# Two layers of long convolution and FFN on one core: k before h at the start, k kept by residue, the first FFN unit started row by row, and a new written-out order

## The chip, the cores and the metric

The kernel runs on one core of a Trainium2 chip. The metric is device time in microseconds (us) of one execution; before the change it is 345.2 us, the median of three runs (345.08 to 345.33). The profile below covers 343.4 us of it, from the first to the last instruction; the remaining 1.84 us (345.24 us for the profiled run itself) lie outside the traced span.

## The reference

The input is a sequence of 2048 rows of 512 bf16 values. Two identical layers follow each other; each has an H3 convolution block (A) and a gated FFN (B), both with a layer norm in front and a residual around them:

```python
def _A_ref(q, k, v, shift_k, ssm_k, ssm_D):
    ...
    for t in range(ks):                       # ks = 4 taps
        k_shift = k_shift + k_pad[:, t:t + S, :] * shift_k[:, ks - 1 - t][None, None, :]
    kv = k_shift * v
    # y = causal convolution of kv with ssm_k over all 2048 rows, per channel, by FFT
    ...
    y = y + kv * ssm_D[None, None, :]
    return q * y
def _B_ref(x, w_gate, w_up, w_down):
    return (_silu(x @ w_gate) * (x @ w_up)) @ w_down     # 512 -> 1792 -> 512

x = A_q
x = x + _A_ref(_layernorm(x), A_k, A_v, A_shift_k, A_ssm_k, A_ssm_D)
x = x + _B_ref(_layernorm(x), B_w_gate, B_w_up, B_w_down)
x = x + _A_ref(_layernorm(x), A_k, A_v, A_shift_k, A_ssm_k, A_ssm_D)
x = x + _B_ref(_layernorm(x), B_w_gate, B_w_up, B_w_down)
```

The convolution's result y doesn't depend on x, so it is computed once and used in both layers.

## The kernel before, in words

**Tiling.** The 2048 rows are cut into four blocks of 512. In a block, partition p holds the rows 4p to 4p + 3; the last of these four numbers is the "residue" r. The convolution is done block by block with a transform of length 1024 whose matrices `fwd` and `inv` (sines and cosines) are made on the chip. A block of h (`ssm_k`) and a block of kv go through matmuls with `fwd` into spectra (`ev`, `G`, `H` for h; `X` for kv), VectorE multiplies spectra (`product`), and matmuls with `inv` bring the sum back to rows (`inverse`, `inverse_half` for block 0). The FFN works on units of two residues of one block, 256 rows: 16 units over both layers. A unit's gate and up matmuls take 14 column tiles of 128 with a moving operand of 256 rows, in groups of 4, 4, 4 and 2 tiles; each pair of tiles fills one PSUM bank `pf`, which ScalarE empties (SiLU for the gate, a copy for the up half). VectorE multiplies the two, and matmuls with `wd` add up in `pd`.

**The start, before the first FFN unit.** Everything here belongs to block 0 and to what must be ready for the first unit:

- SyncE issues the loads: h of block 0 (`hn`, `load_h`), then k (`kn`, `load_k`), v, x, h of block 1, v of block 1 and the gate weights. The taps come through ScalarE's queue.
- VectorE makes the phases `ph`, ScalarE takes their sine into `fwd`, and both, with GpSimd, make the 16 diagonal matrices `dg` (identity times one tap).
- TensorE turns h (`transpose_h`, L476, 16 transposes) and k (`transpose_k`, L365, 16 transposes). The turned k goes from PSUM into `kTb` (L371 on ScalarE, L373 on VectorE), where row 4p + r of the block lies at column 4p + r.
- `shift_mul` (L310 with `kTb` and `dg`, 64 matmuls of 128 columns) makes the shifted k; it reads every fourth column of `kTb`. VectorE multiplies by v (L523).
- TensorE transforms h (`half`, L310 with `hs`) and kv (`direct`, L457); ScalarE and VectorE empty the banks (L418, L421). VectorE forms the products (L641, L645) and the sums `m` (L790); TensorE goes back (L796).
- `prologue(0, 0, 0, True)`: VectorE multiplies the normed x by y (L902, L905), adds it to x (L907), takes the statistics of both rows (L808 to L811), GpSimd raises to the power -1/2 (L813), VectorE normalises (`z`, L863), TensorE turns each row (L919, `ptz`), and ScalarE (row 0, L924) and VectorE (row 1, L922) copy it to `zT`. A statistics tile serves both rows, so the power waits for both.
- Then the first unit's gate and up matmuls start. They read both rows of `zT`.

Work of block 1 (h's transposes and spectrum, the shifted k, the spectrum of kv) is put between these on TensorE as a filler.

**What sets the order.** Each operation is registered with `add` on one engine, with a cost and the buffers it reads and writes. `ORDER` holds a rank for each of them; `Plan.order` sorts by rank, deals out ring slots from modelled times, and `Plan.issue` emits in that order. So each engine's program is in the order of the table, and a wrong guess of a cost can't reorder it on the chip. PSUM is in three rings: `pf` 4 banks, `pc` 2, `pd` 2. The ring `pf` serves the spectra, the turned rows, two of the four rows that come back from the inverse, and the gate and up tiles. Where the model sees TensorE idle for more than 0.5 us early on, `issue` puts in dummy matmuls (`wm`).

Of the kernel before, what the change touches and what calls it, by code (L numbers as in the profile page):

```python
# [29 lines left out]
LH0 = 3.6  # L30
LK0 = 4.3
HQ = 'taps'
# [4 lines left out]
KTE = "ADAD"  # L37
# [5 lines left out]
H_SPLIT = False  # L43
PWA = 2.4
# [6 lines left out]
ORDER = [0, 5, 63, 1, 9, 7, 2, 10, 3, 6, 4, 8, 12, 16, 13, 11, 14, 15, 17, 19, 18, 24, 20, 22, 25, 29, 30, 41, 21, 26, 31, 38, 45, 35, 43, 32, 55,  # L51
         42, 51, 64, 74, 59, 71, 100, 104, 70, 76, 23, 27, 28, 37, 53, 39, 65, 44, 36, 34, 50, 58, 69, 72, 47, 40, 33, 46, 56, 62, 48, 61, 49, 60,
         57, 66, 54, 67, 52, 88, 116, 150, 236, 155, 73, 84, 85, 89, 93, 79, 80, 82, 83, 86, 75, 77, 91, 94, 98, 90, 96, 97, 99, 102, 87, 81, 92,
         101, 95, 106, 110, 144, 170, 165, 185, 109, 113, 105, 107, 112, 111, 114, 118, 103, 108, 68, 78, 115, 120, 119, 123, 139, 130, 121, 124,
         127, 125, 129, 132, 140, 142, 148, 134, 138, 141, 154, 158, 161, 136, 146, 152, 117, 122, 128, 126, 133, 137, 143, 145, 160, 147, 173, 178,
         168, 163, 177, 174, 151, 156, 131, 135, 176, 180, 162, 189, 164, 183, 169, 175, 205, 211, 149, 172, 218, 222, 190, 202, 153, 157, 159, 166,
         179, 195, 167, 171, 188, 197, 182, 184, 186, 187, 192, 194, 207, 225, 199, 209, 198, 248, 216, 191, 204, 196, 203, 206, 200, 208, 210, 214,
         215, 219, 226, 230, 237, 224, 228, 233, 231, 241, 246, 256, 249, 258, 262, 275, 274, 280, 277, 283, 287, 291, 296, 292, 298, 299, 302, 309,
         313, 318, 319, 323, 245, 239, 252, 261, 255, 257, 271, 265, 201, 213, 221, 212, 223, 229, 181, 193, 217, 220, 227, 250, 326, 329, 294, 301,
         285, 289, 235, 244, 238, 284, 312, 324, 264, 268, 293, 305, 332, 339, 345, 347, 354, 350, 330, 232, 242, 438, 300, 279, 310, 320, 328, 336,  # L60
         358, 367, 388, 400, 418, 408, 424, 433, 452, 448, 459, 470, 463, 467, 466, 471, 486, 491, 530, 534, 472, 483, 535, 529, 561, 600, 612, 638,
         234, 240, 251, 263, 259, 270, 243, 260, 254, 267, 276, 304, 286, 247, 253, 266, 272, 278, 282, 281, 303, 306, 321, 317, 273, 311, 297, 308,
         290, 295, 269, 288, 315, 327, 333, 314, 322, 307, 316, 325, 331, 335, 334, 338, 343, 359, 352, 361, 340, 351, 337, 344, 362, 368, 370, 348,
         357, 360, 371, 363, 380, 374, 383, 394, 406, 402, 356, 376, 378, 391, 389, 401, 382, 395, 405, 411, 414, 393, 407, 398, 410, 415, 422, 420,
         426, 423, 429, 341, 346, 342, 349, 353, 364, 365, 366, 369, 372, 375, 379, 384, 381, 385, 387, 390, 396, 399, 403, 404, 409, 444, 458, 441,
         456, 462, 464, 474, 476, 478, 484, 489, 497, 492, 499, 503, 505, 517, 526, 514, 518, 436, 447, 446, 451, 428, 445, 425, 430, 481, 510, 494,
         450, 477, 455, 469, 460, 473, 475, 490, 500, 522, 516, 480, 501, 442, 457, 468, 487, 434, 439, 506, 533, 528, 502, 509, 488, 520, 524, 537,
         539, 546, 544, 551, 685, 580, 386, 419, 435, 461, 449, 482, 485, 511, 504, 519, 531, 555, 559, 542, 554, 560, 563, 571, 574, 581, 585, 437,
         496, 397, 413, 498, 513, 540, 527, 545, 548, 578, 589, 590, 593, 604, 607, 631, 667, 616, 618, 377, 373, 412, 355, 432, 421, 443, 427, 532,
         550, 562, 565, 493, 495, 508, 523, 521, 525, 541, 553, 453, 465, 507, 512, 572, 567, 610, 597, 583, 605, 632, 622, 536, 479, 440, 392, 538,  # L70
         591, 602, 599, 629, 623, 416, 595, 431, 454, 515, 614, 626, 635, 640, 658, 662, 651, 645, 690, 694, 720, 723, 697, 703, 727, 730, 698, 701,
         708, 719, 706, 716, 734, 741, 733, 736, 752, 747, 771, 767, 762, 764, 692, 417, 696, 816, 650, 643, 655, 670, 665, 684, 688, 715, 781, 777,
         788, 792, 814, 800, 822, 830, 837, 861, 866, 869, 874, 880, 875, 879, 894, 896, 876, 882, 889, 892, 888, 893, 904, 937, 923, 942, 954, 948,
         961, 966, 973, 984, 1000, 1037, 557, 569, 547, 556, 573, 579, 564, 568, 586, 596, 624, 587, 598, 603, 611, 592, 606, 577, 584, 619, 634,
         639, 543, 549, 570, 575, 552, 558, 566, 576, 594, 637, 659, 601, 609, 582, 588, 617, 646, 666, 649, 669, 677, 680, 683, 630, 647, 648, 654,
         656, 661, 636, 642, 664, 672, 678, 641, 657, 627, 633, 613, 625, 608, 644, 660, 681, 686, 663, 673, 620, 628, 653, 671, 615, 621, 676, 687,
         691, 674, 679, 668, 675, 682, 689, 695, 693, 699, 702, 704, 709, 710, 721, 722, 732, 700, 712, 742, 770, 761, 735, 753, 729, 738, 749, 756,
         717, 726, 759, 786, 779, 744, 750, 754, 768, 740, 748, 758, 763, 773, 790, 783, 774, 780, 766, 784, 787, 793, 796, 797, 801, 804, 705, 711,
         707, 713, 714, 718, 725, 724, 728, 731, 739, 745, 737, 746, 751, 755, 760, 765, 769, 772, 776, 807, 812, 810, 813, 820, 823, 829, 835, 832,
         842, 844, 848, 852, 850, 854, 856, 858, 865, 870, 878, 868, 872, 839, 845, 819, 825, 824, 831, 799, 827, 815, 821, 834, 860, 863, 828, 838,  # L80
         805, 811, 847, 851, 836, 853, 859, 867, 871, 802, 806, 809, 817, 855, 864, 833, 840, 873, 881, 886, 849, 862, 841, 846, 877, 895, 890, 907,
         917, 1054, 946, 743, 778, 782, 789, 785, 791, 795, 826, 883, 900, 908, 915, 918, 911, 919, 922, 925, 936, 938, 941, 940, 950, 885, 891, 898,
         920, 929, 930, 965, 976, 972, 981, 988, 994, 999, 1001, 1003, 1009, 1018, 1021, 1034, 1045, 1036, 1040, 757, 652, 794, 775, 803, 808, 798,
         818, 843, 857, 979, 986, 978, 982, 910, 914, 901, 913, 897, 905, 884, 887, 947, 951, 991, 996, 1004, 1010, 1013, 1007, 1029, 1015, 997,
         1041, 963, 1025, 983, 955, 1061, 969, 1055, 1069, 927, 1052, 1066, 1035, 1022, 1064, 1068, 1085, 1093, 1113, 1098, 1105, 1118, 1142, 1144,
         1148, 1153, 1147, 1151, 1181, 1185, 1168, 1172, 1155, 1158, 1170, 1173, 1174, 1179, 1160, 1162, 1188, 1195, 1199, 1204, 1208, 1202, 1110,
# [24 lines left out]
R = 4  # L111
# [126 lines left out]
def kernel(  # L238
# [168 lines left out]
    def spectrum(name):  # L407
        return new("s8", name, [P, 4, 2, D], parts=8)
# [878 lines left out]
```

## Time and profile before

| what | value |
|---|---|
| time | 345.2 us (345.08 to 345.33) |
| span of the profile | 343.4 us |
| TensorE busy | 338.5 us, 99% |
| VectorE busy | 279.8 us, 81% |
| ScalarE busy | 254.1 us, 74% |
| GpSimd busy | 38.9 us, 11% |
| gate and up matmuls, 896 + 896 | 111.0 + 110.9 us |
| down matmuls, 462 | 105.5 us |
| granted TensorE clock | 1.000 |

A matmul's row in the profile lasts from its start to its modelled end, and the next one starts before that end. Eight gate matmuls of 256 columns are listed as 1.04 us, yet the next group starts 0.87 us after the first began. So what a matmul costs is read from the distance of starts, not from the sum of durations: 0.109 us for 256 columns, 0.216 us for 512, 0.056 us for 128. The same holds to a lesser degree for the other engines: a VectorE operation listed with 0.41 us may be followed by the next 0.34 us after its start. For the order of things at the start, the timeline of each engine and the busy time in chosen stretches are used.

### The profile page before, as it was taken

To read this page: it belongs to the slowest core of one execution; us is meant where nothing else is said; L and a number is where in the kernel's file an instruction comes from. 1 tells how busy PE (TensorE), PEld (TensorE's weight loads), DVE (VectorE), ACT (ScalarE), POOL (GpSimd) and SP (SyncE) were. 2 spreads that over 40 slices of the span, in tenths; PEclk is the share of its full clock that TensorE was granted. 3 is DMA by queue.
4 is the path that set the end of the run, shared out by engine and by line. 5 is a ranking of instruction groups with operands and counts; after the bars stand their busy time and mean duration, and the time that the engine had idled before them with its cause. 6 is when DMAs were issued, how large, how long until landed. Compare 5 with 4: busy or idle time off the path is not lost.

```text
span 343.4 us, 6604 instructions
## 1 busy us (share of the span) xinstructions
PE 338.5 (99%) x2616; PEld 248.2 (72%) x2616; DVE 279.8 (81%) x479; ACT 254.1 (74%) x503; POOL 38.9 (11%) x46
## 2 busy tenths in 40 slices
PE   8999999999999999999999999999999999999996
PEld 6656868777588657778587767767686877777683
DVE  8899999999999997999999999979998524535112
ACT  7999988989888538977699997569774635556362
POOL 4100110102111001212020001111101000100000
PEclk9999999999999999999999999999999999999999
DMA  7999212091110154132101020510102120101100
GB/s 273 325 298 313 47 31 63 15 166 34 34 46 17 40 95 113 26 63 67 32 10 38 2 76 2 128 26 1 32 0 50 27 36 0 25 8 27 41 12 32
DMA packets 42089, 22.96 MB, mean 67 GB/s; under 512 B 33861, under 2 KB 39882, under 8 KB 42058
## 3 DMA queue, kind: packets, MB, share of 16 engines
q1 hardware_dynamic: 41904, 22.47, 26.5%
q8 instruction: 20, 0.33, 0.4%
q14 instruction: 11, 0.09, 0.1%
q10 hardware_dynamic: 154, 0.07, 0.1%
HBM read 12.33 MB, written 2.10 MB: 42 GB/s over the span
## 4 chain that ended last, share of the span: by engine, by line
PE 96%; ACT 1%; DMA 1%; SPq 0%; issue 0%
PE pf L310 57%; PE pd L985 28%; PE ps L310 7%; PE ps L457 2%; DMA kn<-in_A_k_dram 1%; PE ps L796 1%; PE pd L944 1%; ACT X L418 0%; PE pt L365 0%; ACT hs L486 0%; ACT H L418 0%; PE ptz L919 0%; ACT n L858 0%; SPq L341 0%; PE pt L476 0%; ACT xc L998 0%
## 5 line engine op out<-in xcount | busy, mean ns | idle before, releaser
L310 PE MATMUL pf<-zT,wg_sb 128*128 128x256 bf16 x896 | 111.0, 273 | 0.0
L310 PE MATMUL pf<-zT,wu_sb 128*128 128x256 bf16 x896 | 110.9, 273 | 0.0
L985 PE MATMUL pd<-wd_sb,ht 128*128 128x512 bf16 (+1 forms) x462 | 105.5, 373 | 0.0
L310 PEld LDWEIGHTS <-wu_sb 128*128 128x128 bf16 x896 | 87.7, 98 | 17.4
L310 PEld LDWEIGHTS <-wg_sb 128*128 128x128 bf16 x896 | 87.7, 98 | 16.3 <-issue 0.3
L965 ACT ACTIVATE sg<-pf 128x512 bf16<-128x512 f32 x112 | 65.3, 603 | 24.3 <-PE pf L310 20.3
L969 ACT CAST ht<-pf 128x512 bf16<-128x512 f32 x112 | 65.0, 594 | 23.5 <-PE pf L310 19.8
L985 PEld LDWEIGHTS <-ht 128*128 128x128 bf16 x462 | 45.2, 98 | 42.7
L972 DVE TENSOR_TENSOR ht<-ht,sg 128x1024 bf16<-128x1024 bf16 (+1 forms) x64 | 39.3, 620 | 24.8 <-ACT ht L969 17.3
L813 POOL TENSOR_TENSOR rstd<-ve,nhalf 128x2 f32<-128x2 f32 x24 | 27.7, 1156 | 206.6 <-DVE ve L811 206.6
L808 DVE BATCH_NORM_STATS2 bnst<-xc 128x6 f32<-128x512 bf16 x48 | 31.5, 684 | 1.9 <-ACT xc L1011 1.3
L1021 ACT CAST dn<-pd 128x512 bf16<-128x512 f32 x24 | 13.5, 594 | 21.5 <-PE pd L985 21.5
L1024 DVE TENSOR_TENSOR xc<-xc,dn 128x1024 bf16<-128x1024 bf16 x12 | 8.3, 689 | 18.7 <-ACT dn L1021 18.5
L652 DVE TENSOR_TENSOR t<-X,G 128x2048 bf16<-128x2048 bf16 x18 | 21.9, 1216 | 0.1
L656 DVE TENSOR_TENSOR t<-X,G 128x2048 bf16<-128x2048 bf16 x18 | 21.9, 1217 | 0.0
L418 ACT ACTIVATE X<-ps 128x512 bf16<-128x512 f32 x32 | 19.0, 610 | 1.3 <-PE ps L457 0.7
L418 ACT ACTIVATE H<-ps 128x512 bf16<-128x512 f32 x24 | 13.9, 607 | 1.7 <-PE ps L310 1.5
L839 POOL TENSOR_TENSOR rstd<-ve,nhalf 128x2 f32<-128x2 f32 x8 | 7.7, 958 | 64.8 <-ACT ve L837 64.8
L664 DVE TENSOR_TENSOR t<-t,t 128x2048 bf16<-128x2048 bf16 x12 | 14.7, 1221 | 0.1
L666 DVE TENSOR_TENSOR Z<-Z,t 128x2048 bf16<-128x2048 bf16 x12 | 14.6, 1219 | 0.1
L310 PE MATMUL ps<-hs,fwd 128*128 128x512 bf16 x40 | 12.5, 379 | 0.3 <-ACT H L418 0.3
L603 ACT ACTIVATE ka<-kTb,tapF 128x512 bf16<-128x512 bf16 x16 | 12.4, 787 | 0.0
(109 smaller groups left out, 325.5 us busy)
## 6 DMA issues: line engine op xcount, KB each, us to landing
hn<-in_A_ssm_k_dram SPq DMA_DIRECT2D x4, 512.0 KB, 6.0
vt<-in_A_v_dram SPq DMA_DIRECT2D x4, 512.0 KB, 6.4
xc<-in_A_q_dram SPq DMA_DIRECT2D x4, 512.0 KB, 3.7
out_dram<-xc SPq DMA_DIRECT2D x15, 128.0 KB, 1.8
wg_sb<-in_B_w_gate_dram SPq DMA_DIRECT2D x1, 1792.0 KB
wu_sb<-in_B_w_up_dram SPq DMA_DIRECT2D x1, 1792.0 KB, 8.2
wd_sb<-in_B_w_down_dram SPq DMA_DIRECT2D x1, 1280.0 KB, 11.7
kn<-in_A_k_dram SPq DMA_DIRECT2D x1, 512.0 KB, 4.5
```

The lines of the kernel that those rows point to most:

```text
L310: nc.tensor.matmul(o, lhsT=lhsT, rhs=rhs, start=(n == 0), stop=(n == len(terms) - 1))
L418: add("ACT", act(D), lambda: nc.scalar.activation(out=view(), in_=ps.t[:], func=ACT.Copy, scale=scale), r=[ps], w=[(buf, keys)], conv=conv)
L652: dve(n * D, lambda t1=t1, part=part: nc.vector.tensor_mul(out=t1.t[:], in0=x.t[:, sl, 0, :], in1=g.t[:, sl, part, :]), [(x, key(slots, (0 ...
L656: dve(n * D, lambda t2=t2, part=part: nc.vector.tensor_mul(out=t2.t[:], in0=x.t[:, sl, 1, :], in1=g.t[:, sl, 1 - part, :]), [(x, key(slots ...
L664: dve(n * D, lambda t1=t1, t2=t2, comb=comb: nc.vector.tensor_tensor(out=t1.t[:], in0=t1.t[:], in1=t2.t[:], op=comb), [t2], [t1], conv=conv)
L666: dve(n * D, lambda t1=t1, part=part: nc.vector.tensor_add(out=z.t[:, sl, part, :], in0=z.t[:, sl, part, :], in1=t1.t[:]), [t1], [zk], con ...
L808: add("DVE", 0.6, lambda st=st, i=i: nc.vector.bn_stats(out=st.t[:], in_=xs[c].t[:, i, :]), r=[(xs[c], (i,))], w=[st])
L813: add("POOL", pw, lambda: nc.gpsimd.tensor_tensor(out=rstd.t[:], in0=ve.t[:], in1=nhalf.t[:].to_broadcast((P, n)), op=ALU.pow), r=[ve, nha ...
L965: add("ACT", act(D), lambda ps=ps, o=o, sg=sg: nc.scalar.activation(out=sg.t[:, o:o + 2, :], in_=ps.t[:], func=ACT.Silu), r=[ps], w=[(sg, ...
L969: add("ACT", act(D), lambda ps=ps, o=o, ht=ht: nc.scalar.copy(out=ht.t[:, o:o + 2, :], in_=ps.t[:]), r=[ps], w=[(ht, (o // 2,))], due=(uni ...
L972: dve(n * W, lambda sg=sg, ht=ht: nc.vector.tensor_mul(out=ht.t[:], in0=ht.t[:], in1=sg.t[:]), [sg], [ht], due=(unit, k / pairs, 0.0, "h"))
L985: nc.tensor.matmul((pds[o] if not cs.start else pds[HP]).t[:, cs], lhsT=ht.t[:, q, o * P:(o + 1) * P], rhs=wt["d"].t[:, ft, cs], start=(ft ...
```

## The change

It has four parts, all but the last in the first 33 us of the kernel.

1. **k first.** `HQ = 'tapsk'`: SyncE issues k's load, then h's. k is turned ahead of h.
2. **k by residue.** `kTb` of block 0 becomes [128, 4, 4, 129]: for each residue its 128 rows in a run, with one zero column ahead. The copies out of PSUM become straight copies without a stride, and all four go to VectorE (`KTE = 'DDDD'`; before, two were on ScalarE). The 64 matmuls read a run of 128 columns instead of every fourth.
3. **The first FFN unit row by row.** The statistics of the two rows in the first prologue are split (`PST = True`): a tile, a variance and a power for each row. In the first unit alone, the first four PSUM tiles (`FS = 4`) of gate and up are each made in two halves of eight matmuls, one for each row (128 columns instead of 256), which wait only for their own row of `zT`.
4. **A new order.** Several costs in `add` are changed (they move nothing by themselves), and `ORDER` is a new table for all 1577 operations (1571 before).

New switches `K_SPLIT`, `VE_DVE`, `H1E`, `YD` and the branch `X0 == "mix"` stay at values that leave the emitted work as it was.

```diff
-LH0 = 3.6
-LK0 = 4.3
-HQ = 'taps'
+LH0 = 4.35
+LK0 = 3.5
+HQ = 'tapsk'
-KTE = "ADAD"
+KTE = 'DDDD'
+FS = 4
+PST = True
...
-ORDER = [0, 5, 63, 1, 9, 7, 2, 10, 3, 6, 4, 8, 12, 16, 13, 11, 14, 15, 17, 19, 18, 24, 20, 22, 25, 29, 30, 41, 21, 26, 31, 38, 45, 35, 43, 32, 55,
...
+ORDER = [0, 6, 55, 1, 2, 5, 11, 13, 3, 8, 4, 10, 16, 19, 9, 12, 14, 15, 17, 23, 18, 21, 20, 22, 24, 28, 27, 34, 25, 29, 35, 51, 56, 49, 53, 57, 67,
...
-        kT[b] = new("k", "kTb", [P, KD, PADL + L], parts=KD + 1)
-        add("POOL", 0.2, lambda: nc.gpsimd.memset(kT[b].t[:, :, 0:PADL], 0.0), w=[(kT[b], (KD,))], due=-48)
+        kT[b] = new("k", "kTb", [P, KD, R, P + 1], parts=KD + 1)
+        add("POOL", 0.2, lambda: nc.gpsimd.memset(kT[b].t[:, :, :, 0:1], 0.0), w=[(kT[b], (KD,))], due=-48)
...
-            dst = lambda dt=dt: kT[b].t[:, dt, PADL:PADL + L].rearrange("d (p r) -> d p r", r=R)
-            src = lambda pt=pt: pt.t[:].rearrange("d r p -> d p r")
+            dst = lambda dt=dt: kT[b].t[:, dt, :, 1:P + 1]
+            src = lambda pt=pt: pt.t[:]
...
+            def at(dt, s):
+                if b:
+                    return kT[b].t[:, dt, PADL + s:PADL + s + R * (P - 1) + 1:R]
+                return kT[b].t[:, dt, s % R, 1 + s // R:1 + s // R + P]
...
-                    mm(ps.t[:, dt * P:(dt + 1) * P],
-                       [(kT[b].t[:, dt, PADL + r - j:PADL + r - j + R * (P - 1) + 1:R], dg.t[:, dt, j, :])
-                        for j in range(KS)])
+                    mm(ps.t[:, dt * P:(dt + 1) * P], [(at(dt, r - j), dg.t[:, dt, j, :]) for j in range(KS)])
...
-        st = ln_stats(c, rows, 0.85)
+        sts = [ln_stats(c, [i], 0.85) for i in rows] if PST else [ln_stats(c, rows, 0.85)] * HP
...
-            zop = normalise(z, (0,), lambda z=z: z.t[:], c, i, o, st)
+            zop = normalise(z, (0,), lambda z=z: z.t[:], c, i, 0 if PST else o, sts[o])
...
+                    split = unit == (0, 0, 0) and 2 * k + (which == "u") < FS
+                    ps = new("pf", "pf", [P, D], F32, parts=HP)
+
+                    def part(ps=ps, o=o, which=which, fts=fts, i=0):
+                        for q in (0, 1):
+                            ft = fts[o + q]
+                            mm(ps.t[:, q * W + i * P:q * W + (i + 1) * P],
+                               [(wt[which].t[:, kd, ft * P:(ft + 1) * P], zT.t[:, kd, i]) for kd in range(KD)])
...
+                    if split:
+                        for i in range(HP):
+                            add("PE", pe(2 * KD, P), lambda part=part, i=i: part(i=i), r=[(zT, (i,)), wt[which]], w=[(ps, (i,))], due=due)
+                    else:
+                        add("PE", pe(2 * KD, W), go, r=[zT, wt[which]], w=[ps], due=due)
...
-            h0 = load_h(0, "SP", -70)
-            k0 = load_k(0, -69.9, after=[h0])
+        else:
+            k0 = load_k(0, -70)
+            h0 = load_h(0, "SP", -69.9, after=[k0])
+            k0 = h0
```

Matched to the operations in the order of registration, the two tables give these programs for TensorE at the start (`hT`, `kT`: four transposes each; `H`: two matmuls of 512 columns; `conv rX dtY`: four of 128):

```text
before: hT r1, r2, r0, r3 | kT 0, 1, 3, 2 | H a1, a0, b1, c1 | conv r0 dt0, r2 dt0, r2 dt1, r1 dt0-3, r0 dt1-3, r3 dt0, r2 dt2-3, r3 dt1-3 | H c0, b0 | X ...
after:  kT 0, 3, 1 | hT r2, r0, r3 | kT 2 | hT r1 | H b0, a0, a1 | conv r2 dt0, r1 dt0, r0 dt0-1, r3 dt0, r1 dt1, r3 dt1, r0 dt2-3, r1 dt2-3, r3 dt2, r2 dt1-3, r3 dt3 | H c0, c1, d0 | X ...
```

and these ahead of the first FFN matmuls (`conv1`: 16 of 128; `id`: x added through the identity; `X1`: spectrum of the next block):

```text
before: ... conv1 r3, inverse s1 r2p1, zT1, zT0, id0, X1, X1, id1 | g 0.2, g 1.0, g 0.0, u 0.2 ...
after:  ... conv1 r3, id0, inverse s1 r2p1, zT0, id1, zT1, X1, X1 | g 0.2 row 0, u 0.2 row 1, g 1.0, u 0.2 row 0, g 0.2 row 1 ...
```

## The prediction

> **What bounds the kernel now.** I read the engines' shares first, then the waits of TensorE, then busy time by stretch, then TensorE's timeline by distance of starts.
>
> The page's shares, and the whole answer to "who waited" for TensorE's matmuls:
>
> ```profile
> PE 338.5 (99%) x2616; PEld 248.2 (72%) x2616; DVE 279.8 (81%) x479; ACT 254.1 (74%) x503; POOL 38.9 (11%) x46
> PE wm L1253 <- DVE wz L1037: 1.1, 1, 1.1
> PE ps L310 <- ACT H L418: 0.3, 1, 0.3
> PE pt L365 <- DMA kn<-in_A_k_dram: 0.3, 1, 0.3
> ```
>
> TensorE is the bound, and it waits only at the start. The change gives it no less to do, so it can win only slots in which TensorE does nothing useful. Where are they? Adding up the distances of starts over the whole timeline, with 0.216, 0.109 and 0.056 us for 512, 256 and 128 columns, leaves nothing unexplained from 33.23 us to the last matmul at about 341 us. All lost slots lie ahead of 33.23. Busy time by stretch (stretch, its length, then busy us of TensorE, its weight loads, VectorE, ScalarE, GpSimd, then clock, DMA share, GB/s):
>
> ```profile
> 5.80:21.75 15.95, 15.95 (x145) 10.20 (x146) 14.39 (x29) 14.63 (x33) 2.41 (x6) 1.00 1.10 304
> 21.75:25.70 3.95, 3.52 (x28) 1.98 (x27) 3.92 (x10) 3.95 (x9) 0.00 (x0) 1.00 1.02 389
> 31.20:33.23 2.03, 1.98 (x18) 0.96 (x15) 2.03 (x5) 2.03 (x6) 0.00 (x0) 1.00 1.58 318
> 33.23:341.00 307.77, 307.19 (x2323) 227.22 (x2322) 250.02 (x405) 224.89 (x443) 33.50 (x30) 1.00 0.19 41
> ```
>
> The useful matmuls from 4.44 (h's first transpose) to 33.23 (first FFN matmul) are 76 of 512 columns and 184 of 128: 76 x 0.216 + 184 x 0.056 = 16.4 + 10.3 = 26.7 us in 28.8 us. So 2.1 us are lost, and TensorE's timeline shows where:
>
> ```profile
> 4.44 1.08 PE L476 MATMUL pt<-ident,hn 128*128 128x128 bf16 x16
> 5.80 1.07 PE L365 MATMUL pt<-ident,kn 128*128 128x128 bf16 x16 [0.28 <-DMA kn<-in_A_k_dram]
> ...
> 8.43 3.74 PE L310 MATMUL ps<-dg,kTb 128*128 128x128 bf16 x64
> 12.01 1.03 PE L310 MATMUL ps<-hs,fwd 128*128 128x512 bf16 x4
> ...
> 23.44 0.28 PE L1253 MATMUL wm<-wz 128*128 128x128 bf16 x2
> 24.02 0.38 PE L310 MATMUL ps<-hs,fwd 128*128 128x512 bf16 x1 [0.30 <-ACT H L418]
> 24.50 0.38 PE L796 MATMUL ps<-m,inv 128*128 128x512 bf16 x1
> ...
> 31.21 0.38 PE L796 MATMUL ps<-m,inv 128*128 128x512 bf16 x1
> 31.62 0.72 PE L919 MATMUL ptz<-ident,z 128*128 128x128 bf16 x8
> ```
>
> (a) 4.44 to 5.80: 16 transposes need 0.9, so about 0.5 goes on waiting for k. (b) 21.75 to 25.7: 0.18 + 0.58 (dummies and a wait for ScalarE) + 0.26 + 0.14 = 1.1 to 1.2, with VectorE (3.92 of 3.95) and ScalarE (3.95 of 3.95) both full. (c) 31.2 to 33.2: 0.2 for z, 0.12, 0.18 before the first gate matmul, 0.5 together. From the last matmul to the span's end is 2.4 us, which the change doesn't touch. So the most it can win is about 2.1 us.
>
> **What the Trainium skill says.** "TensorE: Matmul & The Clock Gate", section "Wait — 56ns, not 53.3ns?": warm matmuls follow each other after N/2.4 GHz + 2.5 ns, 55.6 ns at 128 and 215.7 at 512; the distances above agree. Same page, "Step-by-step: what each phase is for": matmuls stay in program order and only weight loads are pulled ahead, so one waiting matmul holds all behind it; the trace agrees at 24.02. "VectorE: DVE Perf Modes", "Mode 2×_1P — pack two bf16 into one 32-bit read": two results a cycle need 16-bit data of step 1. The strided copy of k and the straight one of h, both from PSUM, agree:
>
> ```profile
> 6.36 0.41 DVE L492 COPY hs<-pt 128x512 bf16<-128x512 bf16 x1
> 6.69 0.67 DVE L373 COPY kTb<-pt 128x512 bf16<-128x512 bf16 x1
> ```
>
> "DMA: Bandwidth & Descriptors", "Queues, rings and completion order": descriptors of one queue are consumed in ring order. h issued at 0.74 is in use at 4.43, k issued at 1.26 at 5.80; swapped, I take k at about 4.3 and h at about 5.8, since both must be through before the second can be used and they are 512 KB each.
>
> **The change part by part.**
>
> *k first.* Until the second load, TensorE can do only transposes. Before these were 16 of h; in the new order 12 of k, since `kT 2` stands behind three groups of h. With the second load at the same 5.8, 4 x 0.056 = 0.22 us more is lost. If h comes 0.2 earlier it is nothing; if its shorter runs make it 0.3 later, 0.5.
>
> From 5.8: 16 transposes of h and 4 of k (1.1), three H pairs (1.3), so the shifted k starts at 8.2 instead of 8.43. Is its input there? VectorE does tapF, neg, dg01, tapT, dg10, two copies of k, dg11, hs r0 (6.7), two dg, kTb 2 (7.4), three dg (8.0), hs r1, kTb 1 (8.7). Group 1 needs dg00 at 8.0, and group 4 (8.87) needs kTb 1 at 8.7 and a semaphore: just in time. The first v product, which needs nine groups of 0.224, comes at 10.3 against 10.20. So VectorE's long chain starts no earlier: four v products end at 13.0, ev c1 (0.64, before done at 9.3) takes it to 13.6, where G starts; before G started at 13.55 after waiting 0.65. The moved ev is hidden in that wait.
>
> *k by residue.* Four copies at 0.34 to 0.41 on VectorE, 1.4 to 1.6, for two at 0.67 there and two on ScalarE (1.07 together). VectorE's wait of 0.87 ahead of 10.20 hides the 0.1 to 0.3; ScalarE's 1.0 only lengthens its wait for x at 9.63 (0.32 before). The 64 matmuls stay at 0.056. Nothing on the path.
>
> *The middle, by the new order.* Chaining the rows' distances through the three programs: X s3 ends at 21.3, the second turn of h1 at 21.7 (before, the same work and one more matmul were done at 21.75). The next matmul, H1 r0, needs ScalarE's copy of h1; ScalarE's list from 12.3 (four ev, seven X at 0.5 to 0.55, the second square 0.84, three small ones 0.8, n1 0.75, h1 0.95) reaches it at about 21.8, so TensorE waits 0.2. With every row at its full listed length ScalarE reaches it at 22.5 and the wait is 0.7; I take 0.2. The sum `m s0+` comes at 21.9, before the inverse wants it at 22.4, and `conv1` r2 and r0 (0.9 each) stand behind it as filler where before there were dummies. VectorE reaches `n*y` at 26.25 (26.43 before). TensorE ends `conv1 r3` and the inverse at 31.0, against 31.43. So of the 1.1 to 1.2 lost in (b) some 0.2 stays: 1.0 won.
>
> *Rows apart.* One more variance on VectorE (0.09 to 0.17) and one more power (0.8 to 1.0 on GpSimd, idle). z0's power is done early, so z follows the v products without the 0.25 wait: z0 at 30.85, z1 ends at 31.6; TensorE waits 0.3 for z0, and after zT1 two X1 pairs fill until row 0 of `zT` is copied (32.2). The first gate half can start at about 32.4. Row 1's copy on VectorE now stands behind two v products (ends 32.65), while the first half runs until 32.85. Of (c) 0.1 is won. Each split tile costs 16 x 0.0558 - 8 x 0.1092 = 0.02, four 0.08; the first tile's SiLU comes later than with one piece, but `pf` tiles are freed just in time (the seventh at 37.7, wanted at 37.9).
>
> *After the first unit* the order is new but the work isn't, and the last stretch above has no slack to win and none lost.
>
> Sum: -1.0 (b) - 0.1 (c) + 0.2 (a) + 0.1 (split) = -0.8 us. **344.4 us.**
>
> **The rivals.**
>
> *A, forecast, 42%:* as above, 344.4.
>
> *B, no change, 30%:* h lands late (+0.5 in (a)) or ScalarE's copy of h1 comes at 22.5 (+0.5). Then the gain in (b) is given back: with one of them -0.8 + 0.5 = -0.3 (344.9), with both -0.8 + 1.0 = +0.2 (345.4). For it: ScalarE is full from 19 to 31 in the trace, and TensorE has no wait to spare.
>
> *C, slower, 20%:* both of B, and the wait is passed on: VectorE is a chain without gaps from 13.55 to 31.15, so a late X or h1 moves z, the 0.7 at h1 pulls behind it H1 and the inverse, and `pf` banks become short in the first unit (0.5 more). -0.8 + 3 x 0.5 = +0.7, 345.9; a new wait of 0.4 after 33 us would make it 346.3. Against it: in the trace a full VectorE never stopped TensorE after 33 us.
>
> *D, all of it, 8%:* nearly all lost slots go and k comes early: -1.8 to -2.0, 343.3.
>
> **How the numbers follow.** The likeliest is A, 344.4. The range leaves out D's end and C's: 343.5 to 346.0. Faster by over 0.2% (below 344.5) are A and D, 0.50; same is B, 0.30; slower C, 0.20.
>
> **What would show it.** Right: TensorE's first FFN matmul near 32.4 and everything after it unchanged; k's transposes at about 4.3 and h's at 5.8; no dummies between 21 and 25, one short wait near 21.8; `kTb` copies at 0.41. Wrong: h landing well after 5.8 and TensorE waiting longer than 0.7 there; matmuls waiting for ScalarE's h1 or H1 by 0.5 or more; any wait of TensorE after 33 us, which would void the claim that only the start matters; or a first FFN matmul that moves while the end doesn't.

## The result, and the profile after

After the change the kernel takes 346.93 us (median of 6 runs, 346.38 to 347.42) against 345.32 us before (6 runs beside it, 345.08 to 346.22). The ratio is 1.0042, 95% interval 1.0028 to 1.0057: it got slower by about 0.4%, where 344.4 us, a gain, was forecast. The profiled spans are 345.4 us after and 343.4 us before.

I read the same views in the same order as before. First the page's shares, and then the whole answer to "who waited" for TensorE's matmuls (us in total, times, longest), now of the kernel after:

```profile
PE 337.5 (98%) x2616; PEld 248.8 (72%) x2649; DVE 277.8 (80%) x482; ACT 252.0 (73%) x501; POOL 39.8 (12%) x47
```

```profile
PE pf L317 <- DMA zT<-z: 1.7, 2, 0.9
PE wm L1305 <- DVE wz L1076: 1.0, 1, 1.0
PE ptz L946 <- DVE z L890: 0.3, 1, 0.3
```

The first of the waits is new, and it is nearly the whole of what was lost: TensorE waits twice for the transfer that turns normed rows into `zT`. The waits for k and for ScalarE's `H` are off this list (the wait for the second load isn't gone: four dummies stand in it, as the timeline below shows). One trap is in the shares: 2649 weight loads but only 2616 matmuls. The 33 missing matmul records show up in the timeline as gaps of one slot (0.22 us, about one every 10 us), in which nothing was lost. They also make TensorE's busy time look smaller than it was.

Busy time by the same stretches as before (stretch, its length, then busy us of TensorE, its weight loads, VectorE, ScalarE, GpSimd, then clock, DMA share, GB/s), kernel after:

```profile
5.80:21.75 15.95, 15.79 (x142) 10.02 (x142) 13.94 (x32) 13.16 (x30) 2.16 (x4) 1.00 1.09 318
21.75:25.70 3.95, 3.86 (x47) 2.92 (x47) 3.92 (x10) 3.95 (x7) 0.00 (x0) 1.00 1.01 395
31.20:33.23 2.03, 1.75 (x21) 1.27 (x21) 2.03 (x7) 2.03 (x7) 0.14 (x1) 1.00 0.70 129
33.23:341.00 307.77, 304.58 (x2311) 225.72 (x2338) 247.77 (x403) 223.79 (x443) 33.78 (x30) 1.00 0.19 41
```

The stretch 21.75 to 25.70 is fuller (3.86 for 3.52), as forecast. The last stretch, where no slot was missing before, has lost 2.6 us of busy time. Part of that is missing records (27 more loads than matmuls in it), so the loss itself has to be read from TensorE's timeline. The start of the kernel after:

```profile
4.14 1.47 PE L379 MATMUL pt<-ident,kn 128*128 128x128 bf16 x12
5.40 0.63 PE L1305 MATMUL wm<-wz 128*128 128x128 bf16 x4
6.09 0.85 PE L494 MATMUL pt<-ident,hn 128*128 128x128 bf16 x12
6.78 0.39 PE L379 MATMUL pt<-ident,kn 128*128 128x128 bf16 x4
7.00 0.39 PE L494 MATMUL pt<-ident,hn 128*128 128x128 bf16 x4
7.33 1.46 PE L317 MATMUL ps<-hs,fwd 128*128 128x512 bf16 x5
8.62 3.74 PE L317 MATMUL ps<-dg,kTb 128*128 128x128 bf16 x64
...
23.50 1.95 PE L317 MATMUL ps<-dg,kTb 128*128 128x128 bf16 x32
25.29 0.38 PE L317 MATMUL ps<-hs,fwd 128*128 128x512 bf16 x1
25.75 0.81 PE L819 MATMUL ps<-m,inv 128*128 128x512 bf16 x3
...
31.64 0.40 PE L946 MATMUL ptz<-ident,z 128*128 128x128 bf16 x4 [0.28 <-DVE z L890]
...
32.75 0.61 PE L317 MATMUL pf<-zT,wg_sb 128*128 128x128 bf16 x8
```

h can be used from 6.09, where before the second load (k) could be used from 5.80. (The first twelve transposes of k start 0.106 us apart, where the transposes of h in the kernel before were 0.056 apart. Nothing is lost by it, since they are done at 5.40, before h has come.) In the middle the 32 matmuls of the shifted k stand where dummies stood, and one wait of 0.24 is left (25.29 to 25.75, less a slot), for VectorE's sum `m`. The first FFN matmul starts at 32.75 instead of 33.23. So at this point the change is 0.48 us ahead, and yet the last matmul of all starts at 342.06 instead of 340.15. The two places where the rest went, in the same view:

```profile
50.05 2.75 PE L1024 MATMUL pd<-wd_sb,ht 128*128 128x512 bf16 x12
53.66 1.05 PE L317 MATMUL pf<-zT,wg_sb 128*128 128x256 bf16 x8 [0.86 <-DMA zT<-z]
...
130.25 0.59 PE L317 MATMUL ps<-vt,fwd 128*128 128x512 bf16 x2
131.66 1.59 PE L317 MATMUL pf<-zT,wg_sb 128*128 128x256 bf16 x13 [0.82 <-DMA zT<-z]
```

Twelve matmuls of 0.216 from 50.05 are done at 52.64, two from 130.25 at 130.68. The next starts at 53.66 and 131.66. By distance of starts TensorE loses 1.03 and 0.98 us. In the kernel before, the matmuls at the same two places follow at once:

```profile
50.20 2.75 PE L985 MATMUL pd<-wd_sb,ht 128*128 128x512 bf16 x12
52.79 1.04 PE L310 MATMUL pf<-zT,wu_sb 128*128 128x256 bf16 x8
...
129.32 0.59 PE L310 MATMUL ps<-vt,fwd 128*128 128x512 bf16 x2
129.75 1.04 PE L310 MATMUL pf<-zT,wu_sb 128*128 128x256 bf16 x8
```

The full account of TensorE in these two traces, by three marks (first spectrum matmul of h, first FFN matmul, last matmul):

| stretch | before | after | difference |
|---|---|---|---|
| to the first `ps<-hs,fwd` | 6.71 | 7.33 | +0.62 |
| from there to the first FFN matmul | 26.52 | 25.42 | -1.10 |
| from there to the last matmul | 306.92 | 309.32 | +2.40 |
| sum (start of the last matmul) | 340.15 | 342.06 | +1.9 |

Of the +2.40, the waits are 1.03 + 0.98. Another 0.33 goes within the first unit (0.08 for the 64 shorter matmuls, and short gaps of 0.06, 0.10 and 0.09 at 38, 43 and 46 us).

### The profile page after: what moved, and what is told of

The parts are those of the page before. It is cut to its first block, busy times and chain, and to the rows that moved or that the text cites. A ratio compares the mean times of both kernels' runs of the same rounds, so it can differ in the third digit from the quotient of the medians.

```text
span 345.4 us, 6633 instructions
## 1 busy us (share of the span) xinstructions
PE 337.5 (98%) x2616; PEld 248.8 (72%) x2649; DVE 277.8 (80%) x482; ACT 252.0 (73%) x501; POOL 39.8 (12%) x47
## 4 chain that ended last, share of the span: by engine, by line
PE 83%; DVE 9%; ACT 3%; DMA 2%; issue 1%; DVEq 0%
PE pf L317 51%; PE pd L1024 25%; PE ps L317 5%; DMA zT<-z 2%; DVE t L664 1%; DVE m L562 1%; PE wm L1305 1%; DVE Z L668 1%; ACT sg L1004 1%; ACT X L436 1%; DVE G L603 1%; PE pt L379 0%; ACT ht L1008 0%; ACT z L885 0%; DVE vt L537 0%
## 5 line engine op out<-in xcount | busy, mean ns | idle before, releaser
L317 PE MATMUL pf<-zT,wg_sb 128*128 128x256 bf16 (+1 forms) x912 | 110.6, 271 | 1.7 <-DMA zT<-z 1.7
L317 PE MATMUL pf<-zT,wu_sb 128*128 128x256 bf16 (+1 forms) x912 | 111.5, 271 | 0.3
L1024 PE MATMUL pd<-wd_sb,ht 128*128 128x512 bf16 (+1 forms) x442 | 101.2, 373 | 1.1
L1008 ACT CAST ht<-pf 128x512 bf16<-128x512 f32 x112 | 63.9, 592 | 21.4 <-PE pf L317 21.2
L1011 DVE TENSOR_TENSOR ht<-ht,sg 128x1024 bf16<-128x1024 bf16 (+1 forms) x64 | 39.4, 620 | 32.4 <-ACT sg L1004 20.4
L836 POOL TENSOR_TENSOR rstd<-ve,nhalf 128x2 f32<-128x2 f32 (+1 forms) x25 | 25.9, 1036 | 213.7 <-DVE ve L834 213.7
L866 POOL TENSOR_TENSOR rstd<-ve,nhalf 128x2 f32<-128x2 f32 x8 | 10.4, 1294 | 59.3 <-ACT ve L864 59.3
L626 ACT ACTIVATE kc<-kTb,tapF 128x512 bf16<-128x512 bf16 x16 | 12.6, 803 | 0.0
```

The source lines that it names most:

```text
L317: nc.tensor.matmul(o, lhsT=lhsT, rhs=rhs, start=(n == 0), stop=(n == len(terms) - 1))
L626: add("ACT", 0.66, lambda j=j, t=t, h=h, dt=dt: nc.scalar.activation(out=t.t[:, h, :, dt], in_=kT[b].t[:, dt, PADL - j:PADL - j + L].rearr ...
L836: add("POOL", pw, lambda: nc.gpsimd.tensor_tensor(out=rstd.t[:], in0=ve.t[:], in1=nhalf.t[:].to_broadcast((P, n)), op=ALU.pow), r=[ve, nha ...
L1008: add("ACT", act(D), lambda ps=ps, o=o, ht=ht: nc.scalar.copy(out=ht.t[:, o:o + 2, :], in_=ps.t[:]), r=[ps], w=[(ht, (o // 2,))], due=(uni ...
L1011: dve(n * W, lambda sg=sg, ht=ht: nc.vector.tensor_mul(out=ht.t[:], in0=ht.t[:], in1=sg.t[:]), [sg], [ht], due=(unit, k / pairs, 0.0, "h"))
L1024: nc.tensor.matmul((pds[o] if not cs.start else pds[HP]).t[:, cs], lhsT=ht.t[:, q, o * P:(o + 1) * P], rhs=wt["d"].t[:, ft, cs], start=(ft ...
```

## What held the second row up: two suspects

The first wait is the strange one. SyncE's queue around it, kernel after:

```profile
48.32 2.50 SPq L919 DMA_TRANSPOSE zT<-z  x2
50.87 1.60 SPq L403 DMA_DIRECT2D xc<-in_A_q_dram  x1
```

The two turns of `zT` (transposed DMA transfers, one for each row of the unit) are issued at 48.32 and 49.6, as before (48.09), and are wanted at 52.64, as before (52.79). The view of times to landing lists only 2.4 us for them, yet TensorE starts at 53.66. What held it up is to be seen in the single packets, from the trace's DMA records of the kernel after (start, duration in us, queue, bytes):

```text
50.656  1.444  q8  instruction  16384
51.395  1.504  q1    256
51.422  1.475  q1    256
51.433  1.466  q1    256
51.499  1.406  q1    256
51.518  1.385  q1      4
...     (13 such packets; the last starts at 51.668; all end at 52.90 to 52.91)
```

The other small packets of this turn have a median of 0.018 us and none takes over 0.06. Thirteen take 1.24 to 1.50 and end together at 52.90, 0.8 us before TensorE starts. The one other transfer that lasts, and that is under way when all of them start, is a fetch of 16 KB of instructions (50.66 to 52.10). "Runtime: NRT & Kernel Launch" of the Trainium skill, section "Instruction fetch mechanics", says that an engine's program comes in blocks of 16 KiB, 256 instructions, over a DMA queue of its own, and that the cost of crossing into the next is "mostly hidden". The trace agrees on the size. The question here is not that cost but what the fetch does to another transfer. The profile's page has 20 such fetches in all. 20 x 256 is close to the 5298 loads and matmuls of TensorE's program, so I take them to be TensorE's. "DMA: Bandwidth & Descriptors" of the same Trainium skill, section "Queues, rings and completion order", says that a DMA engine serves the queues that have work for it in turn, a packet at a time. That fits thirteen packets held up at once on one DMA engine, but the records don't name the engine, so this last step is argued. The traces do tie the packets to the fetch by time. Over all traces of this document there are nine places near 48 and 67 us where packets of a turn take more than 0.2 us. In each of them a fetch of 0.92 to 1.57 us is under way, and the held packets end 0.76 to 0.84 us after the fetch does. What fills these 0.8 us isn't shown. A hold also isn't a loss yet. In the kernel after, the next fetch (68.99 to 69.91) holds packets of the second unit's turn until 70.72 to 70.75, and TensorE loses nothing there.

Before, the fetch in question came at 55.3, after the turn had landed. The change puts 66 more loads and matmuls (64 of the split, one dummy pair) into TensorE's program before this point.

*Theory:* the fetch falls on the turn, and that is the wait at 52.6. In the new order the split brought it there. *Rival:* the new order makes the turn late, and the fetch is a bystander. The wait at 130 seems to have an explanation of its own, in the order of SyncE's queue there, kernel after:

```profile
124.10 2.20 SPq L367 DMA_TRANSPOSE kTb<-in_A_k_dram  x1
126.47 0.45 SPq L403 DMA_DIRECT2D xc<-in_A_q_dram  x1
127.02 1.19 SPq L919 DMA_TRANSPOSE zT<-z  x1
```

z was ready at 122.9, but the turn stands behind two loads and lands 4.6 us after its issue (median of all turns: 2.5). Before, it was issued at 121.16, ahead of both loads (127.43 and 127.81).

## The experiments

A ratio is always to the kernel before, formed from runs beside each other on one chip. It isn't the quotient of the two medians given, which lump rounds together. Where the fetch lies is read from the DMA records. "Lost" is the distance of starts less the matmul's slot.

### The split alone in the old kernel

```diff
 before, with its own order and h first
+FS = 4          (gate and up tiles 0 and 1 of the first unit, a half for each row)
 dummies (29):
-matmul(t[:], lhsT=wz.t[:], rhs=wz.t[:])                         x n
+matmul(t[0:104, 0:104], lhsT=wz.t[:, 0:104], rhs=wz.t[:, 0:104])  x 5n/4
```

> The kernel before with one part of the change, the row-by-row split of the first four gate and up tiles, in the old order; the dummies at the start are 104 columns wide instead of 128 and a quarter more in number, so that they take the same time and TensorE's instruction stream is 76 instructions longer (64 by the split, 12 by the dummies). Theory F: TensorE's 16 KB instruction fetch at 55.3 us moves to about 50.4, onto the transposed load of the second unit's zT (its packets run from 49.2 to 51.5), and TensorE waits 0.3 to 0.9 us for zT near 52.9: 345.7 to 346.3 us. Theory O, that the waits for zT come from the new order alone: no such wait, only the split's 0.1: 345.4 us.

Measured: 345.81 against 345.63, ratio 0.9996 (0.9977 to 1.0016). The fetch came at 54.2, not at the 50 it was steered to, so this run missed its target and can't speak for or against the theory. It does size the split: from the first FFN matmul to the last it is 307.00 us for 306.92, so the shorter matmuls cost 0.08 us, and no wait follows after 33 us.

### The turn ahead of the loads

```diff
 SyncE near 124 us, kernel after, by ORDER:
-kTb <- in_A_k_dram ; xc <- in_A_q_dram ; zT <- z
+zT <- z ; kTb <- in_A_k_dram ; xc <- in_A_q_dram
```

> The changed kernel with one edit in SyncE's order: the transposed load of zT that is issued at 127.0 us, behind the transposed load of k's last block and the load of x, goes ahead of these two. Theory Q, that zT stands in the queue behind the 0.5 MB of k and 0.5 MB of x: the wait of 0.8 to 1.0 us at 130.7 goes, 345.9 to 346.1 us, and the wait at 52.6 stays. Rival, that TensorE arrives there too early for z whatever the queue: the wait stays, 346.9 us.

Measured: 346.86 against 345.63, 1.0033 (1.0019 to 1.0046). The wait at 130 is gone. The wait at 52 stays (1.19; fetch at 51.0), and the traced run has a new one of 0.39 at 71.7, where the next fetch (68.3, 1.57 long) meets the turn of the second unit (issued 67.47). So the wait at 130 goes when the turn goes ahead of the loads, but curing it alone recovers little: the 345.9 to 346.1 expected was missed, and the time is the rival's, though its reason is not.

### The fetch moved, without touching the change

```diff
 dummies of the kernel after:
-t = psp.tile([P, P], ...);      for _ in range(n):             matmul(t[:], lhsT=wz.t[:], rhs=wz.t[:])
+t = psp.tile([P, 2 * P], ...);  for _ in range((n + 1) // 2):  matmul(t[:], lhsT=wz.t[:, 0:P], rhs=wz.t[:])
```

The dummies fill the same time with half as many instructions. A second version has 512 columns and a quarter as many; a third 104 columns and a quarter more, which should bring the fetch forward; a fourth joins the first with the turn ahead of the loads.

> The changed kernel with its early dummies 256 columns wide instead of 128 and half as many, so that TensorE's instruction stream is some 30 instructions shorter. Nothing else changes. Theory F, that the instruction fetch that starts at 50.66 us holds up one DMA engine's part of zT: the fetch comes about 2 us later, the wait of 0.9 to 1.0 us at 52.6 goes, 345.9 to 346.1 us, and the wait at 130.7 stays. Rival, that z is simply made too late for TensorE: the wait stays at 0.5 or more, 346.5 to 346.9 us.

> The changed kernel with both edits: zT ahead of k and x in SyncE's order, and the dummies twice as wide and half as many. Theories F and Q together: no wait for zT over 0.3 us, 344.9 to 345.2 us, slightly below the kernel before, since the first FFN matmul comes 0.5 us earlier and 0.3 us of it is given back in the first unit. If the two waits are passed on to other places: 346 us or more.

> The changed kernel with its early dummies 512 columns wide and a quarter as many, some 44 instructions fewer in TensorE's stream (30 fewer in the run with 256 columns). Theory F: the fetch comes at 55 us or later, no wait for zT near 52.6, and the time is that of the run with 256 columns, 0.4 to 0.5% below the changed kernel. If it was the form of the dummies and not the length of the stream that helped there, the two differ.

> The changed kernel with its early dummies 104 columns wide and a quarter more in number, some 14 instructions more in TensorE's stream. Theory F: the fetch near 50.7 comes about 1 us earlier, 49.5 to 50.5, still on zT's two transposed loads (49.2 to 51.5): the wait stays, 0.4 to 1.0 us, and the time is within 0.15% of the changed kernel. If any change of the dummies removed the wait, it would be gone here too.

> The changed kernel itself, beside the others on one chip, with a second trace. Theory F (the instruction fetch holds up a transposed load of zT): its fetch lies again within 1.5 us of 50.7 us and TensorE waits 0.5 to 1.2 us for zT near 52.6; 0.3 to 0.5% slower than before. If the first trace caught a rare coincidence, no such wait, and the time lies elsewhere.

| version | time, before beside it | ratio (95%) | fetch | lost at 52 | lost at 130 |
|---|---|---|---|---|---|
| after itself, again | 347.40, 345.91 | 1.0034 (1.0018 to 1.0049) | 51.3 | 1.12 | 1.14 |
| dummies 256 wide | 345.40, 345.63 | 0.9988 (0.9976 to 1.0001) | 55.1 | none | 0.64 |
| dummies 512 wide | 345.58, 345.91 | 0.9992 (0.9974 to 1.0009) | 55.3 | none | 0.75 |
| 256 wide, turn first | 345.40, 345.63 | 0.9982 (0.9967 to 0.9997) | 56.1 | none | none |
| dummies 104 wide | 345.86, 345.91 | 1.0003 (0.9988 to 1.0018) | 48.7 | 0.09 | none |

The useful work and its order are the same in the first, second, third and fifth row; only the dummies differ, by 14 to 46 instructions of 5300. The wait at 52 is there with the fetch at 51.3, is down to 0.09 at 48.7, and is absent at 55.1 and 55.3. That shows the theory's first half: the place of the fetch decides. The versions with 256 columns moved the fetch by more than the 2 us expected: alone, the change is 0.5 us below its expectation, while with the turn first, at 345.40, it is just above it (345.2 at most). The 104-wide version missed its expectation (the wait was to stay), and usefully: the fetch came so early that it held twelve packets at the end of the first turn (until 50.64) and was over before the second turn's packets ran. Its trace is of one of the shortest of its twelve runs (344.80, their median 345.86), so it doesn't show what the longer ones lose.

The waits of TensorE with both cures, whole answer:

```profile
PE wm L1304 <- DVE wz L1075: 1.2, 1, 1.2
PE ptz L945 <- DVE z L889: 0.3, 1, 0.3
```

### The split undone

```diff
-FS = 4
+FS = 0
 (each tile at the place of its later half in ORDER; k first, k by residue, statistics by row kept)
 second version, in addition: zT <- z ahead of kTb and xc on SyncE near 124 us
```

> The changed kernel with the split of the first unit's tiles alone undone (FS = 0: each tile in one piece of 256 columns, at the place of its later half); k first, k by residue, statistics by row and the order are kept. TensorE's program has 64 fewer loads and matmuls together ahead of 52 us. Theory (the split's instructions bring TensorE's instruction fetch onto the second row's zT): the fetch lies at 54 to 57 us, the wait at 52.6 is gone, the time is about 345.4 (ratio to before 0.998 to 1.001), and the first FFN matmul starts some 0.4 later than 32.75. Rival (the new order itself brings the wait, wherever the fetch lies): a wait of 0.8 or more at 52 to 54 us stays and the time is 346.5 or more. The wait at 130 is another cause and may stay, 0.6 to 1.0, in both.

> The same without the split, and with SyncE's turn of the second row's zT near 127 us put ahead of the loads of k and x. Theory: no wait at 52 and none at 130; the time is 0.0 to 0.9 below the version without the split alone, about 345.0 (0.997 to 1.000). If the split is worth anything apart from its fetch, this is slower than the version with the fetch moved and the turn first (0.9982) by up to 0.3 us; if it is worth nothing, the same. Rival (order): slower than before, with a wait of 0.8 or more at 52 us.

Measured: 346.21 against 345.75, 1.0018 (1.0010 to 1.0026), and with the turn first 345.47, 0.9997 (0.9989 to 1.0005). TensorE's timeline without the split:

```profile
50.08 2.75 PE L1023 MATMUL pd<-wd_sb,ht 128*128 128x512 bf16 x12
52.67 1.04 PE L316 MATMUL pf<-zT,wg_sb 128*128 128x256 bf16 x8
```

With the split away the fetch is at 55.2 and the gate matmuls follow at once, in the new order. The rival of the first half falls. (In the old order neither the split nor 58 more dummy instructions, below, brought the fetch there: 54.2 and 53.3. So it takes the split together with the rest of the new program.) The first time was above what I expected (1.001 at most), since the wait at 130 was still the full 0.98. The pair of runs sizes that wait, too: its cure takes 1.0018 to 0.9997, 0.7 us, and the intervals don't meet. From the first FFN matmul to the last the second version has 306.92 us, the very figure of the kernel before.

### The fetch alone, without the split

```diff
 dummies of the kernel before, and of the version without the split and with the turn first:
-matmul(t[:], lhsT=wz.t[:], rhs=wz.t[:])                       x n
+matmul(t[0:64, 0:64], lhsT=wz.t[:, 0:64], rhs=wz.t[:, 0:64])  x 2n
```

> The kernel before, with nothing of the change in it: its 29 dummy matmuls of 128 columns at the start become 58 of 64 columns, which is the same time and 58 more loads and matmuls in TensorE's program, close to the 64 that the split adds. Theory (the place of the instruction fetch is enough to cost the time): if the fetch near 50 us falls between 50.6 and 51.3, TensorE waits 0.8 to 1.2 for the second row's zT at 52.8 and the time is above before (1.001 to 1.004); if it falls elsewhere (it did so once in an old-order kernel with such an addition: 54.2), no wait and 0.999 to 1.001. Rival (the wait belongs to the new order, the fetch only happens to lie there): no wait in either case.

> The version without the split and with the turn first (0.9997, no wait after 33 us in its profile), with the dummies likewise 60 of 64 columns in place of 30 of 128. Theory: with the fetch between 50.6 and 51.3 the wait for the second row's zT at 52 is back, 0.8 to 1.2, without any split, and the ratio goes up to 1.001 to 1.004; with the fetch elsewhere no wait and 0.999 to 1.001. Rival (the wait comes from the split's matmuls being slower or from their order): no wait wherever the fetch lies.

Measured: in the old kernel 345.79 against 345.82, 1.0002 (0.9987 to 1.0018), fetch at 53.3, no wait. That again missed the turn. In the other 346.09 against 345.82, 1.0020 (1.0005 to 1.0035). Here the fetch near 50 went to 56.2, but the next one, at 71.6 without the extra dummies, came to 69.5, on the turn of the second unit (issued at 67.08). TensorE's timeline in this version, and then the times to landing of the two turns:

```profile
68.74 2.97 PE L1023 MATMUL pd<-wd_sb,ht 128*128 128x512 bf16 x12
72.47 1.80 PE L316 MATMUL pf<-zT,wg_sb 128*128 128x256 bf16 x15 [0.77 <-DMA zT<-z]
```

```profile
DMA to landing us min/median/max: 2.4/3.2/4.0
```

The same wait (0.93 lost), with the same sign: thirteen packets of 1.27 to 1.54 us that end together at 71.72. It is at another place, for another unit, without the split, in a version that has no wait after 33 us otherwise. The wait that was expected at 52 didn't come, since the fetch missed that turn. The traced run is one of four among twenty with spans of 345.5 or more; the other sixteen lie at 343.5 to 344.6, and the median of all, 344.05, is that of the kernel before (344.0). So the 1.0020 comes from a few long runs, and that the fetch hits in those and not in the others is likely but not shown, since only one was traced.

### h first, the rest kept

```diff
 256-wide dummies and the turn first, and:
-HQ = 'tapsk'
+HQ = 'taps'     (h loaded, turned and copied ahead of k; dg and kTb in a matching order on VectorE)
```

> The changed kernel with zT ahead of k and x in SyncE's order and the dummies 256 wide (the pair of edits that ran at 0.9982 of before), and now h's load first again, with its transposes, copies and the diagonal matrices in the order that suits it; k by residue, the split statistics and the split tiles stay. If k first cost TensorE 0.3 to 0.5 us at the second load, as the trace of the changed kernel says, the first FFN matmul comes at 32.2 to 32.6 and the time falls to 0.9970 to 0.9980 of before. If k first was worth something, it rises above 0.9985.

Measured: 345.45 against 345.91, 0.9983 (0.9968 to 0.9997). The same as with k first (0.9982), so loading k first is worth nothing that can be told apart here. By the marks, the first spectrum matmul comes at 7.02 and the stretch to the first FFN matmul takes 25.78 instead of 25.42. So that matmul comes at 32.80, earlier than in the trace with k first (33.28) and later than the 32.2 to 32.6 expected. The first mark scatters by more than this between traces of one order.

### All traces side by side

Columns: first spectrum matmul; from it to the first FFN matmul; from there to the last matmul; how long after the issue of the two `zT` turns near 48 and near 67 us a fetch starts; what TensorE loses at 52, 71 and 130.

| kernel | spectrum | to FFN | to the last | fetch after issue, 48 / 67 | lost 52 / 71 / 130 |
|---|---|---|---|---|---|
| before | 6.71 | 26.52 | 306.92 | 7.2 / 6.4 | - / - / - |
| before, 64-wide dummies | 6.39 | 26.64 | 306.92 | 5.4 / 6.7 | - / - / - |
| before with split | 6.58 | 26.51 | 307.00 | 6.2 / -0.1 | - / - / - |
| after | 7.33 | 25.42 | 309.32 | **2.3** / 1.5 | 1.03 / - / 0.98 |
| after, again | 7.53 | 25.42 | 309.74 | **2.8** / 0.7 | 1.12 / - / 1.14 |
| turn first | 7.17 | 25.42 | 308.83 | **2.9** / 0.8 | 1.19 / 0.39 / - |
| 256 wide | 7.33 | 25.42 | 307.93 | 6.8 / 5.0 | - / - / 0.64 |
| 512 wide | 7.23 | 25.42 | 308.04 | 7.0 / 5.1 | - / - / 0.75 |
| 104 wide | 6.84 | 25.42 | 307.34 | 0.9 / -0.8 | 0.09 / - / - |
| 256 wide, turn first | 7.86 | 25.42 | 307.31 | 7.2 / 4.9 | - / - / - |
| the same, h first | 7.02 | 25.78 | 307.28 | 7.2 / 4.9 | - / - / - |
| no split | 7.33 | 25.78 | 307.92 | 6.8 / 5.4 | - / - / 0.98 |
| no split, turn first | 6.93 | 25.79 | 306.92 | 7.0 / 5.5 | - / - / - |
| the same, 64 wide | 7.93 | 25.78 | 307.85 | 7.3 / **2.4** | - / 0.93 / - |

In 14 traces a turn loses about 1 us in the four places where a fetch starts 2.3 to 2.9 us after its issue, and at most 0.39 for all the other turns near 48 and 67 us. The third column is 306.92 to 307.00 without waits under the old start or without the split, 307.3 with the split in the new order, and more only by the waits listed.

The table's last column also shows that the order of SyncE's queue isn't the whole cause of the wait at 130. The 104-wide version has the same order and loses nothing there: its turn is issued at 124.31, lands 4.7 us later at 129.0, and TensorE wants it at 129.19. In the five traces that do lose time at 130, a fetch that starts at 119.5 to 122.2 overlaps the issue of one transposed transfer in this queue, and that issue takes 0.8 to 1.2 us longer than its like in the 104-wide version (2.18 and 2.25 instead of 1.19, 2.06 instead of 1.26, 3.06 and 3.11 instead of 1.89), whose fetch is at 116.65. So the queue alone leaves the turn just in time, and a fetch seems to make it late. This is argued: no run moved that fetch alone, the issue that took 1.89 there takes up to 2.65 in other versions without a fetch on it, and in the h-first version a fetch at 120.37 lengthened the transposed transfer under it by nothing (1.26).

## Why the prediction was wrong

The step that failed is this one: "After the first unit the order is new but the work isn't, and the last stretch above has no slack to win and none lost." The work after the first unit was indeed the same. But two transfers came later, or were held up, by up to 1 us each, and TensorE has no reserve there: 1.03 + 0.98 = 2.0 us. The forecast judged the order after 33 us only by TensorE's work and by full engines. It didn't chain each transfer of `zT` from its issue to its landing through SyncE's new queue. The risk at 130 us could have been seen: SyncE's program is in the order of the table, and the table puts the turn behind two loads. The cause at 52 could be suspected only with the fetches in view.

*(a) The second load.* Put at +0.2, with +0.5 as the bad end. It was +0.62 in the pair of traces: h arrives 0.29 later than k did; behind it come 20 transposes instead of 16 (0.22); and 0.1 is lost between the last of them and the spectrum. The mechanism named was right, the term too small. The forecast's "shifted k starts at 8.2" became 8.62. This mark scatters from trace to trace: 6.39 to 6.71 in the three with h first and the old order, 6.84 to 7.93 in the ten with k first (means 6.56 and 7.35).

*(b) The middle.* Put at -1.0: one wait of 0.2 should stay, near 21.8, for ScalarE's copy of h1. There only 0.06 was lost; the 0.24 that stayed is at 25.5, for VectorE's `m`, so that the size of what stays is nearly right by luck. By distance of starts (b) lost 1.15 before and 0.30 after, a gain of 0.85. *(c) Before the FFN.* Put at -0.1. It lost 0.47 before and 0.23 after, the wait for the first row's `z`, a gain of 0.24. Together (b) and (c) were put at -1.1, and the stretch from the spectrum to the first FFN matmul shortened by 1.10: the sum is right because the two errors cancel. The first FFN matmul, forecast at 32.4, came at 32.75, later by what (a) was too small by. `kTb`'s copies took the 0.41 forecast:

```profile
L391 DVE COPY kTb<-pt x4: 410/414/425, 5.2 to 8.6; 128x512 bf16<-128x512 bf16 x4
```

*The split.* Put at +0.1 in matmul time; the old kernel with the split shows 0.08. In the new order it costs 0.33 to 0.39 after the first FFN matmul. It wins 0.36 ahead of it (25.78 without, 25.42 with), so nothing stays. What was missed altogether is that 64 more instructions also move TensorE's program against its fetches.

So without the two waits the sum would have been +0.62 - 1.10 + 0.39 = -0.1 instead of -0.8. With them it is +1.9, which is what the spans show (+2.0). The versions cured of both waits say the same from the other side: 0.9982, 0.9983 and 0.9997 of before, a gain of 0 to 0.2%. Rival C had the sign but not the place: it let a late h1 and short `pf` banks pass the wait on. Only its last clause, "a new wait of 0.4 after 33 us", and the line that such a wait "would void the claim that only the start matters" met the case, and with them the last sign named there, a first FFN matmul that moves (0.48 earlier) while the end doesn't follow.

**What stays open.** Which instruction count triggers a fetch: the one near 50 us comes with the 926th to the 998th load or matmul of the traces, and 58 to 60 more dummy instructions made it 2.0 us earlier in one version and 1.3 us later in another (1.0 of it since the first FFN matmul came later). So I could steer it, but not aim. That the held packets lie on the fetch's own DMA engine is argued from their common end. And moving the fetch gained 0.3 to 0.5% in the runs (1.5 to 1.8 us between medians of runs beside each other), as much as or somewhat more than the 1.4 us between the two traces of the kernel after and of the 256-wide version (342.06 and 340.68): more of the wait at 130 and of other turns may hang on it.

The best versions run here are the change with 256-wide dummies and the turn first (345.40) and the same with h first (345.45). By their ratios both are 0.2% below the kernel before (0.9982 and 0.9983).

## What to carry to other kernels

Where a kernel has no slack after its start, don't argue a new order by the work on the busiest engine. Chain each small transfer that a later stage waits for, from issue to landing, and see what stands ahead of it in its queue. After a change that adds or removes instructions on the fullest engine, look at where its 16 KB instruction fetches now fall, and test a doubtful loss by shifting them with a few dummies: if the loss vanishes, it was not the change's own logic. And give a late consumer's transfer 1 to 2 us of room (TensorE lost up to 1.2 us here), since no table of durations will show such a meeting.

## What the runs showed that I had not expected

A single 16 KB instruction fetch, 1.0 to 1.5 us long in the four places where it cost most and there about every 17 us, held up twelve or thirteen of 1088 small packets for 1.2 to 1.6 us each, and thereby a transfer that the whole of TensorE waited for (0.93 to 1.19 us in four traces). The held packets end together some 0.8 us after the fetch. Taking away 30 to 46 dummy instructions of 5300 was worth 0.4 to 0.5% of the time. And matmul records can be missing: 33 of 2649 here, at even distances, each looking like a lost slot of 0.22 us. Comparing the number of weight loads with that of matmuls gives them away.
